# TensorE's matmuls of the head loop in the order of emission, with a head's preparation, maxima and loads moved up

## The chip, the cores and the metric

The kernel runs on one core of a Trainium2 chip. Its engines are TensorE (PE; PEld is its weight load), VectorE (DVE), ScalarE (ACT), GpSimd (POOL) and SyncE (SP), which issues the DMAs here. The metric is the device time of one execution in microseconds (us). Three runs of the kernel before took 1082.86, 1084.32 and 1095.21 us; the median is 1084.32.

## The reference

Three layers follow one another. All inputs are float32; B = 4 batches, H = 8 heads, S = 1152 positions, D = 64.

```
# 1. attention with pooled queries
q_pool = q.reshape(B, H, S // 2, 2, D).mean(axis=3)          # 576 queries a head
attn   = softmax(q_pool @ k^T / 8)                           # sum + 1e-9
x      = (attn @ v), heads side by side                      # (4, 576, 512)
# 2. four attention experts, each token uses two of them
logits = x @ w_gate;  the two largest, softmax over the two
ye     = causal_softmax((x wq[e]) (x wk[e])^T / 8) @ (x wv[e]) @ wo[e]
x      = sum over the two chosen e of weight * ye
# 3. token mix and feed-forward
xk, xr = mu * x + (1 - mu) * x_prev
out    = sigmoid(xr @ w_r) * (relu(xk @ w_k)^2 @ w_v)
```

## The kernel before, in words

**Precision.** Most products are taken in `float32r` with each operand split into a high and a low part (`_h`, `_l`), so one product is three matmuls, or two where high and low parts are stacked along the 128 contraction rows.

**Stage 1, a head.** A head hh (32 of them, eight to a batch) has these pieces.
- `s1_load` (L590 to L598): two DMAs bring q (`qr`, L596) and k (`kr`, L597) into one buffer each.
- `s1_prep` (L610 to L719): POOL adds the query pairs (`qp`, L625); TensorE transposes k (L635, five matmuls) and q (L681, three) into PSUM; ACT or DVE copy the high part out, DVE computes the low part; two steps later eight DMAs lay the parts into KA, KB and QB (L670 to L672, L711). KA, KB, QA and QB have three copies, so head hh + 3 takes over those of head hh.
- `s1_max` (L721 to L742): 15 matmuls of 384 columns (L728), each into a PSUM bank that DVE reduces at once (L730); then `max_finish` (L394 to L405): DVE reduces to `nm` (L397), TensorE transposes it (L402), DVE copies it out (L403) and a DMA on SP (L404) writes it as a row of QB, where the second score matmul subtracts it.
- `s1_job` (L744 to L820): nine steps. The part `qk` of a step is four score matmuls of 288 columns (L758, L759, two pairs) into one of two PSUM tiles `st`; ACT takes the exponential (L766), for two steps of three a copy splits it (L64) and DVE computes the rest (L71). Four steps later the part `pv` multiplies with V (L786, or L793 to L795).
- `s1_vload`, `s1_vsplit`: V is loaded (L602) and split.

**Stage 2, an expert** of the batch before is woven into the heads of the next batch: `s2_vproj`, `s2_qk` (tile `stq`, L348), `s2_max` (L422, L427, five atoms and a `max_finish`), `s2_job` (three steps, scores L467 and L468, products L496) and `s2_out`. They stand as additional steps between those of a head; the positions `p1` to `p6` and `po` in the dictionary G fix where.

**What sets the order.** `drive` (L176 to L206) walks through the 353 steps of the head loop. In step i it emits `qk` of step i, its exponential, the low part of step i - 2, and then, in the gaps before, between and after the `pv` parts of step i - 4, what the tasks have due. A task has a start and an end, both counted in steps, and a list of atoms; `Task.run` emits as many atoms as the elapsed share of the window asks for. Preparation, maxima, loads and the rest are such tasks; their windows come from G (`pr0`, `mx0`, `ld` and others), where x below zero counts from the first step of a head backward. `later(n, f)` emits f at the end of the n-th step from now: `G["nm"]` and `G["nm2"]` are that n for the transposition of the maxima of a head and of an expert.

What is emitted so is a program order only. When the program is compiled, the framework's scheduler simulates the engines and lets an engine take a later instruction where the first in line isn't ready in that simulation. The order in which each engine's queue then stands is fixed; at run time each queue goes through it in that order. PSUM has two tiles `st` of two banks, and four banks (`aux()`) for everything else: transpositions, maxima and the accumulators of the products.

After the head loop a second `drive` (L1274) computes the last batch's experts, and stage 3 follows.

Of the kernel before, what the change touches and what calls it, by code (L numbers as in the profile page):

```python
# [22 lines left out]

P = 128
D = 64
G = {'LAG': 4, 'LO': 2, 'nf1': 2, 'nfx': 1, 'mxA': (0, 5), 'prA': (0.5, 5.0), 'mx0': (-2.0, 7.0), 'mx1': (-2.5, 6.0), 'vl': (0.0, 1.5), 'vs': (5.5, 1.0), 'pr0': (0.5, 5.0), 'pr1': (0.5, 4.0), 'ld': (6.5, 5.5), 'm2': (2.0, 1.5), 'nm': 0, 'nm2': 0, 'dup': 2, 'mid': 1, 'bc': 1, 'end': 9, 'mid2': 2, 'end2': 4, 'spl': 9, 'gate': 8, 'gate2': 2, 'w2': (2, 30), 'w3': (7, 14), 'S0': ('n', 'sv', 'sv', 'n', 'sv', 'sv', 'n', 'sv', 'sv'), 'S1': ('n', 'sv', 'sv', 'n', 'sv', 'sv', 'n', 'sv', 'sv'), 've': 'g', 'kh0': 's', 'kh1': 'v', 'qh0': 's', 'qh1': 's', 'kq': 's', 'kl': 'v', 'rs': 'v', 'rl': 'v', 'ym': 'g', 'yo': 'v', 'LGe': 'v', 'p1': (5, 5, 5, 9), 'p2': (9, 9, 9), 'p3': (2,), 'p4': (9, 9, 9, 9), 'p5': (8, 8, 8, 8), 'p6': (9, 9, 9), 'po': (2, 4, 5, 9), 'add0': 'g', 'add1': 'g', 'xt': 'v', 'u1': 's', 'u2': 's', 'y2': 'v', 'yh': 's', 'yl': 'v', 'xo': 'v', 'v2': 's', 'xh': 's', 'xl': 'v', 'vvh': 's', 'vvl': 'g', 'klo': 'v', 'HB': 3, 'PB': 6, 'blk': 1, 'm2w': 2, 'order': 2, 'kdup': 0, 'L2': 4, 'O2': 1, 'a0': (5.0, 5.0), 'a1': (2.0, 2.5), 'a2': (0.0, 1.0), 'a3': (2.0, 2.0), 'r0': 2, 'NV': 2, 'NF': 2, 'SA': ('n', 'vg', 'sg', 'n', 'sv', 'n', 'sv', 'sv', 'sv'), 'SB': ('n', 'sv', 'sv', 'n', 'vv', 'n', 'sv', 'sv', 'sv'), 'ua': 'v', 'u0': 's', 'xt0': 'v', 'w3d': 8, 'w3q': (3, 27), 'WC': 1, 'kb': 1, 'kst': 1, 'qst': 0, 'CW': 512, 'wt': 'v', 'wl': 'v', 'wa': 'v', 'WB': 1, 'mxg': 2, 'hq': 's', 'hpos': (0, 1, 11, 20)}
NEG = -1.0e30

TINY = 1.17e-9
# [26 lines left out]
def tile_kernel(ctx: ExitStack, tc: tile.TileContext, q, k, v, w_gate, wq, wk, wv, wo,  # L56
                mu_k, mu_r, w_k, w_v, w_r, out):
    nc = tc.nc
    LAG, LO, HB = G["LAG"], G["LO"], G["HB"]
    eng = {"g": nc.gpsimd, "v": nc.vector, "s": nc.scalar}  # L60

    def copy(e, dst, src):
        if e == "s":
            nc.scalar.activation(dst, src, AF.Copy)  # L64
        elif e == "v":
            nc.vector.tensor_copy(dst, src)
        else:
            nc.gpsimd.tensor_scalar(dst, src, 1.0, 0.0, op0=ALU.mult, op1=ALU.add)

    def lo_of(e, dst, src, hi):  # L70
        eng[e].tensor_tensor(dst, src, hi.bitcast(F32), op=ALU.subtract)  # L71
# [82 lines left out]
    def later(n, fn):  # L154
        pending.append((now[0] + n, fn))

    def run_later(everything=False):
        while pending:
            x = min(pending, key=lambda x: x[0])
            if x[0] > now[0]:  # L160
                if not everything:
                    return
                now[0] = x[0]
            pending.remove(x)
            x[1]()
# [3 lines left out]
    def drive(steps, tasks, drain=False):  # L169
        def fill(t):  # L170
            for x in tasks:
                x.run(t)

        for i, st in enumerate(steps):
            now[0] += 1
            if st.qk:  # L176
                st.qk()
            if st.ew:
                st.ew()
            lagged.append(st)  # L180
            if len(lagged) > LO and lagged[-1 - LO].ew2:
                lagged[-1 - LO].ew2()
                lagged[-1 - LO].ew2 = None
            pv = lagged.pop(0).pv if len(lagged) > LAG else ()
            m = len(pv) + 1
            for j in range(m):
                fill(i + (j + 1) / m - 1e-6)
                if j < len(pv):
                    pv[j]()
            run_later()  # L190
        if drain:
            for st in lagged:
                if st.ew2:
                    st.ew2()
                    st.ew2 = None
            while lagged:
                for f in lagged.pop(0).pv:
                    f()
                now[0] += 1
                run_later()  # L200
            run_later(True)
# [36 lines left out]
    def normaliser(U, gate, name):  # L238
# [8 lines left out]
        def mid():  # L247
# [3 lines left out]
            nc.sync.dma_start(scr.rearrange("o (p i) -> (o p) i", p=D), rd)  # L251
            later(G["bc"], bcast)

# [6 lines left out]
    def s2_split(b):  # L260
        def one(p):
            def f():
                copy(G["xh"], XH[:, p], XT[:, p])
                lo_of(G["xl"], XL[:, p], XT[:, p], XH[:, p])
            return f
        return [one(p) for p in range(NP)]

    def s2_vproj(b):
        W = E * D + E

        def make(cs):
# [13 lines left out]
            def ew():  # L285
                for j, c in enumerate(cs):
                    n = TC[c][1]
                    copy(G["v2"], V2[:n, c, :, 0:D], cell["st"][:n, j, : E * D].rearrange("p (e d) -> p e d", e=E))

# [7 lines left out]
    def s2_gate(b):  # L297
# [3 lines left out]
        def f():  # L301
# [22 lines left out]
            def g():  # L324
# [9 lines left out]
                nc.sync.dma_start(GR, gscr.rearrange("e (p i) -> p e i", p=D))  # L334
            later(G["gate2"], g)
        return [f]
# [230 lines left out]
    NK, NV = 3, G["NV"]  # L567

    order = sorted(range(NK), key=lambda i: (i - (B * H)) % NK)
# [6 lines left out]
    NF = G["NF"]  # L576
# [13 lines left out]
    def s1_load(hh):  # L590
        b, h = hh // H, hh % H
        kr = s1a.tile([P, NC * D], F32, tag="kr", name=f"kr{hh}")
        qr = s1a.tile([QW, NQ, 2, D], F32, tag="qr", name=f"qr{hh}")
        raw[hh] = kr, qr
        return [
            lambda: nc.sync.dma_start(qr, q[b, h].rearrange("(c p r) d -> p c r d", p=QW, r=2)),  # L596
            lambda: nc.sync.dma_start(kr, k[b, h].rearrange("(p c) d -> p (c d)", p=P)),  # L597
        ]  # L598

    def s1_vload(hh):  # L600
        b, h = hh // H, hh % H
        return [lambda: nc.sync.dma_start(VF[hh % NF][:, :, 0:D], v[b, h].rearrange("(p c) d -> p c d", p=P))]  # L602
# [116 lines left out]
    def s1_max(hh):  # L719
        i = hh % NK  # L720
        pm = PM[hh % 2]  # L721

        def one(c, g):
            t0, n = TC[c]

            def f():
                ps = aux()
                nc.tensor.matmul(ps[:n, : 3 * P], QA[i][:, t0 : t0 + n], KA[i][:, 3 * g * P : 3 * (g + 1) * P],  # L728
                                 start=True, stop=True)
                nc.vector.tensor_reduce(pm[:n, c, g : g + 1], ps[:n, : 3 * P], axis=AX.X, op=ALU.max)  # L730
            return f

        def some(a, z):
            return [one(c, g) for c in range(a, z) for g in range(3)]

        if hh >= G["nfx"]:
            return some(0, len(TC)) + [lambda: max_finish(pm, QB[i], f"1_{hh}")]

        m = -(-HT // P)
        return some(0, m) + [lambda: first_max(pm, QB[i], 0, m)] + \  # L740
            some(m, len(TC)) + [lambda: first_max(pm, QB[i], m, len(TC))]
# [119 lines left out]
    CW = G["CW"]  # L861
# [68 lines left out]
    steps, tasks = [], []  # L930
# [16 lines left out]
    def at(hh, x):  # L947
        if x < 0:
            return at_[hh][0] + x
        if x >= NC:  # L950
            return at_[hh][NC - 1] + x - NC + 1
        return at_[hh][int(x)] + x - int(x)
# [23 lines left out]
    for hh in range(3):  # L976
        for a in s1_load(hh):
            a()
        if hh < 2:
# [3 lines left out]
            if hh == 0:  # L983
                mx = s1_max(0)
# [7 lines left out]
    for hh in range(NH):  # L992
        z = "0" if hh < H else "1"
        if hh + 1 < NH:
            mx = G["mx" + z] if hh else G["mxA"]
            e = at(hh, mx[1])
            if G["mxg"] and ex_[hh] and hh >= H:
                e = max(e, at_[hh + 1][0] - G["mxg"])
            tasks.append(Task(at(hh, mx[0]), e, s1_max(hh + 1)))
            a = LAG + G["vl"][0]  # L1000
            tasks.append(Task(at(hh, a), at(hh, a + G["vl"][1]), lambda hh=hh: s1_vload(hh + 1)))
            a = LAG + G["vs"][0]
            tasks.append(Task(at(hh, a), at(hh, a + G["vs"][1]), lambda hh=hh: s1_vsplit(hh + 1)))
        if hh + 2 < NH:
            pr = G["pr" + z] if hh else G["prA"]
            tasks.append(Task(at(hh, pr[0]), at(hh, pr[1]), lambda hh=hh: s1_prep(hh + 2)))
        if hh + 3 < NH:
            tasks.append(Task(at(hh, G["ld"][0]), at(hh, G["ld"][1]), lambda hh=hh: s1_load(hh + 3)))
    if G["order"]:
        tasks = tasks[::-1] if G["order"] == 1 else sorted(tasks, key=lambda t: t.start) if G["order"] == 2 else sorted(tasks, key=lambda t: t.end)  # L1010
    n = len(steps)
# [57 lines left out]
    tasks.append(Task(n - 7, n - 6, [wk_open]))  # L1069
    tasks.append(Task(n - 6, n - 5, [lambda: s3_mix(0, "xk")]))  # L1070
    tasks.append(Task(n - 5, n - 1, [wk_part(kt, j) for kt in range(KT) for j in range(2)]))
    drive(steps, tasks, drain=True)
    ph1.close()


# [137 lines left out]
    LAG, LO = G["L2"], G["O2"]  # L1213
    flow, tasks = [], []
# [16 lines left out]
    steps, ix = [], []  # L1231
# [70 lines left out]
```

## Time and profile before

| | |
|---|---|
| median of three runs | 1084.32 us |
| the profiled execution | 1088.18 us |
| its span, from the first to the last instruction | 1086.4 us |
| mean granted TensorE clock | 0.981 |
| TensorE busy | 1024.2 us, 94% |
| DVE busy | 821.5 us, 76% |
| ACT busy | 577.4 us, 53% |
| POOL busy | 192.6 us, 18% |

The profile is of one execution. The time of the execution holds 1.8 us around the span. A busy share says how much of the span an engine had an instruction in work; matmuls overlap, so two of them that start 0.13 us apart can each be shown with 0.3 us. What ended an engine's idle time is inferred from semaphores; where the named instruction was long done, it was another one. The granted clock is a share of 2.4 GHz.

### The profile page before, as it was taken

Reading aid. Unit: us, or ns where it says so; the run is one execution under the profiler, and the core shown is the slowest. Engines: PE = TensorE matmul, PEld = TensorE weight load, DVE = VectorE, ACT = ScalarE, POOL = GpSimd, SP = SyncE. Lnnn points to the kernel's source line nnn. Section 1 sums busy time; section 2 is a strip of 40 time slices with the busy share of each in tenths; the row PEclk is TensorE's granted clock in tenths of the full one; section 3 lists DMA queues with packets and bytes.
Section 4 is the critical chain, followed back from the end, with each engine's and each line's share of the span. In section 5 each row is a group of like instructions: output and inputs, shape, how many; then the busy total and the mean of one; then the engine's idle time right before and its main releaser. Section 6 shows DMA issues by size and latency. Waiting matters only on the chain.

```text
span 1086.4 us, 18206 instructions
## 1 busy us (share of the span) xinstructions
PE 1024.2 (94%) x6480; PEld 891.5 (82%) x6480; DVE 821.5 (76%) x1753; ACT 577.4 (53%) x1011; POOL 192.6 (18%) x277
## 2 busy tenths in 40 slices
PE   5999999999999999999999999998898899999998
PEld 4788988888888888888788888878776688888886
DVE  5898999789899989898898897875876635444442
ACT  4567777457676555766655576663555212222222
POOL 6431121021121112112111111121021001111110
PEclk9899999999999999999999999999898899999999
DMA  4555555455554644644464444157255311111100
GB/s 112 140 138 129 131 133 135 103 120 131 135 126 101 171 117 118 152 124 122 102 164 128 109 120 93 42 171 227 83 181 151 102 42 40 39 40 39 39 21 20
DMA packets 129096, 119.24 MB, mean 110 GB/s; under 512 B 63751, under 2 KB 91358, under 8 KB 129006
## 3 DMA queue, kind: packets, MB, share of 16 engines
q1 hardware_dynamic: 129006, 118.08, 41.7%
q8 instruction: 51, 0.84, 0.3%
q14 instruction: 39, 0.32, 0.1%
HBM read 63.24 MB, written 20.07 MB: 77 GB/s over the span
## 4 chain that ended last, share of the span: by engine, by line
PE 61%; DVE 14%; DMA 13%; ACT 6%; issue 3%; SPq 1%; POOL 0%; DVEq 0%; ACTq 0%; POOLq 0%
PE stw L1135 9%; PE sth L1099 7%; PE bank L728 6%; PE bank L786 5%; PE st L758 5%; PE st L759 5%; PE str L1122 4%; PE stq L348 4%; DMA R<-scr 4%; DVE PM L730 3%; PE bank L795 3%; PE bank L794 3%; PE bank L793 3%; PE bank L496 3%; DMA w3l<-w3st 2%
## 5 line engine op out<-in xcount | busy, mean ns | idle before, releaser
L730 DVE TENSOR_REDUCE PM<-bank 128x1 f32<-128x384 f32 (+1 forms) x480 | 252.5, 544 | 19.5 <-PE bank L728 16.6
L766 ACT ACTIVATE p<-st 128x576 f32<-128x576 f32 x288 | 184.5, 647 | 120.4 <-PE st L759 114.3
L728 PE MATMUL bank<-KA,QA 128*128 128x384 f32 (+1 forms) x480 | 187.6, 403 | 12.0 <-DVE KB L145 4.4
L758 PE MATMUL st<-QA,KA 128*128 128x288 f32 x576 | 177.4, 319 | 3.6 <-ACT p L766 2.7
L759 PE MATMUL st<-QB,KB 65*128 65x288 f32 x576 | 169.0, 309 | 0.1
L71 DVE TENSOR_TENSOR pl<-p,ph 128x576 fp32r<-128x576 f32 x190 | 142.9, 754 | 6.2 <-ACT ph L64 5.3
L64 ACT ACTIVATE ph<-p 128x576 fp32r<-128x576 f32 x190 | 129.6, 684 | 19.9 <-PE bank L794 6.3
L758 PEld LDWEIGHTS st<-QA,KA 128*128 128x128 f32 x576 | 111.9, 195 | 15.5 <-ACT p L766 6.9
L786 PE MATMUL bank<-p,VF 128*65 128x288 f32 x384 | 118.3, 406 | 0.3
L793 PE MATMUL bank<-ph,VV 128*65 128x288 f32 x384 | 116.9, 305 | 0.1
L759 PEld LDWEIGHTS st<-QB,KB 65*128 65x128 f32 x576 | 111.4, 195 | 4.1 <-DMA QB<-mr 0.9
L728 PEld LDWEIGHTS bank<-KA,QA 128*128 128x128 f32 (+1 forms) x480 | 87.3, 185 | 33.2 <-DVE PM L730 8.0
L795 PE MATMUL bank<-pl,VV 128*65 128x288 f32 x384 | 113.8, 296 | 0.0
L794 PE MATMUL bank<-ph,VV 128*64 128x288 f32 x384 | 113.7, 296 | 0.0
L1099 PE MATMUL sth<-xkh,wk 128*128 128x256 f32 x512 | 91.4, 279 | 1.2 <-ACT relu L1106 1.2
L1106 ACT ACTIVATE relu<-sth 128x512 f32<-128x512 f32 x32 | 17.5, 596 | 123.2 <-PE sth L1099 122.5
L1099 PEld LDWEIGHTS sth<-xkh,wk 128*128 128x128 f32 x512 | 78.8, 188 | 1.8 <-ACT relu L1106 1.4
L625 POOL TENSOR_TENSOR qp<-qr 96x384 f32<-96x384 f32 x31 | 37.7, 1217 | 239.7 <-PE bank L681 160.4
L482 POOL TENSOR_SCALAR_AFFINE_SELECT p<-p 128x128 f32<-128x128 f32 (+1 forms) x96 | 36.4, 411 | 204.6 <-ACT p L474 192.9
L1099 PE MATMUL sth<-xkl,wk 128*128 128x256 f32 x256 | 71.5, 279 | 0.0
L71 POOL TENSOR_TENSOR VV<-VF,VV 128x576 fp32r<-128x576 f32 x32 | 44.5, 1390 | 146.2 <-ACT VV L64 92.8
L1107 DVE TENSOR_TENSOR relu<-relu 128x512 f32<-128x512 f32 x32 | 20.9, 688 | 57.9 <-ACT relu L1106 57.9
(205 smaller groups left out, 2275.8 us busy)
## 6 DMA issues: line engine op xcount, KB each, us to landing
KA<-sk SPq DMA_DIRECT2D x60, 160.0 KB
qr<-in_q_dram SPq DMA_DIRECT2D x32, 288.0 KB
kr<-in_k_dram SPq DMA_DIRECT2D x32, 288.0 KB
VF<-in_v_dram SPq DMA_DIRECT2D x32, 288.0 KB
KA<-sk SPq DMA_DIRECT2D x60, 128.0 KB
R<-scr SPq DMA_DIRECT2D x48, 144.0 KB
w3h<-w3st SPq DMA_DIRECT2D x20, 256.0 KB
w3l<-w3st SPq DMA_DIRECT2D x20, 256.0 KB
```

The costliest lines, as they stand in the source:

```text
L64: nc.scalar.activation(dst, src, AF.Copy)
L71: eng[e].tensor_tensor(dst, src, hi.bitcast(F32), op=ALU.subtract)
L728: nc.tensor.matmul(ps[:n, : 3 * P], QA[i][:, t0 : t0 + n], KA[i][:, 3 * g * P : 3 * (g + 1) * P], start=True, stop=True)
L730: nc.vector.tensor_reduce(pm[:n, c, g : g + 1], ps[:n, : 3 * P], axis=AX.X, op=ALU.max)
L758: nc.tensor.matmul(st[:, n, :HT], KA[i][:, ks], QA[i][:, cs], start=True, stop=False)
L759: nc.tensor.matmul(st[:, n, :HT], KB[i][0 : D + 1, ks], QB[i][0 : D + 1, cs], start=False, stop=True)
L766: nc.scalar.activation(pt, st[:, :, :HT], AF.Exp, scale=1.0 / 16.0)
L786: nc.tensor.matmul(a[: D + 1, :HT], VF[hh % NF][:, c], cell["p"][:, n], start=c == 0, stop=c == NC - 1)
L793: nc.tensor.matmul(a[: D + 1, :HT], vh, ph[:, n], start=c == 0, stop=False)
L794: nc.tensor.matmul(a[:D, :HT], vl, ph[:, n], start=False, stop=False)
L795: nc.tensor.matmul(a[: D + 1, :HT], vh, pl[:, n], start=False, stop=c == NC - 1)
L1099: nc.tensor.matmul(st[:, f // 2, f % 2 * GT : (f % 2 + 1) * GT], w[kt][:, fs], x[:, kt], start=i == 0, stop=i == 3 * KT - 1)
```

## The change

Two things change. First, the head loop's `drive` stands inside `tc.manual_schedule(engines={PE})`: the scheduler keeps TensorE's instructions of that loop in the order of emission. The other engines are scheduled as before, and so is all that comes before and after the loop. Second, windows in G move, and the first three heads get windows of their own.

```diff
-    'mx0': (-2.0, 7.0), 'mx1': (-2.5, 6.0),
+    'mx0': (-4.5, 4.5), 'mx1': (-4.5, 4.5), 'mxB': (-1.0, 5.5), 'mxC': (-3.5, 5.0),
-    'pr0': (0.5, 5.0), 'pr1': (0.5, 4.0),
+    'pr0': (-3.0, 1.0), 'pr1': (-3.0, 1.0), 'prB': (-1.5, 2.0),
-    'ld': (6.5, 5.5),
+    'ld': (1.5, 1.0), 'ldA': (5.5, 5.0), 'ldB': (2.5, 2.0),
-    'm2': (2.0, 1.5), 'nm': 0, 'nm2': 0,  'mxg': 2,
+    'm2': (2.0, 3.0), 'nm': 1, 'nm2': 1,  'mxg': 4,
...
-            mx = G["mx" + z] if hh else G["mxA"]
+            mx = G["mx" + z] if hh > 2 else G["mx" + "ABC"[hh]]
...
-            pr = G["pr" + z] if hh else G["prA"]
+            pr = G["pr" + z] if hh > 1 else G["prB"] if hh else G["prA"]
...
-            tasks.append(Task(at(hh, G["ld"][0]), at(hh, G["ld"][1]), lambda hh=hh: s1_load(hh + 3)))
+            ld = G["ld"] if hh > 1 else G["ldB"] if hh else G["ldA"]
+            tasks.append(Task(at(hh, ld[0]), at(hh, ld[1]), lambda hh=hh: s1_load(hh + 3)))
...
-    drive(steps, tasks, drain=True)
+    with tc.manual_schedule(engines={mybir.EngineType.PE}):
+        drive(steps, tasks, drain=True)
```

Worked out from the windows and `drive`, the pieces of a head are emitted so many steps ahead of its own first score step (a head of batch 0, heads 5 to 8; and, for later batches, where additional steps stand between, the range):

| piece | before, batch 0 | after, batch 0 | before, later | after, later |
|---|---|---|---|---|
| loads | 21 | 26 | 25 to 32 | 30 to 37 |
| preparation, first to last | 18 to 15 | 21 to 18 | 21 to 26, 18 to 23 | 24 to 29, 21 to 26 |
| its DMAs | 14, 13 | 17, 16 | 17 to 22 | 20 to 25 |
| first maximum | 11 | 14 | 12 to 16 | 14 to 18 |
| last maximum | 4 | 6 | 4 or 5 | 6 |
| transposition of the maxima | 3 | 5 | 3 or 4 | 4 or 5 |

For an expert the maxima end a step earlier, and their transposition stays at the same step, three before the expert's first scores.

## Rows read from the trace of the kernel before

**Rows 1.** The page, part 1: busy time and share of the span by engine.
```profile
PE 1024.2 (94%) x6480; PEld 891.5 (82%) x6480; DVE 821.5 (76%) x1753; ACT 577.4 (53%) x1011; POOL 192.6 (18%) x277
```

**Rows 2.** Windows: length; busy (count) of PE, PEld, DVE, ACT, POOL; clock, DMA.
```profile
0.00:34.90 34.90, 22.04 (x84) 17.75 (x85) 19.63 (x49) 18.84 (x41) 22.67 (x36) 0.91 0.47 110
34.90:98.30 63.40, 58.90 (x368) 50.32 (x367) 56.54 (x114) 38.87 (x70) 18.88 (x20) 0.97 0.60 144
98.30:180.40 82.10, 81.23 (x541) 72.27 (x540) 78.16 (x158) 60.93 (x108) 14.04 (x10) 1.00 0.51 125
180.40:715.50 535.10, 518.67 (x3436) 451.89 (x3435) 472.80 (x1073) 336.00 (x596) 83.05 (x112) 0.99 0.49 121
```

**Rows 3.** Groups by line; after the bar busy us, mean ns, idle before.
```profile
L758 PE MATMUL st<-QA,KA 128*128 128x288 f32 x576 | 177.4, 319 | 3.6 <-ACT p L766 2.7 <-DVE QA L145 0.5
```

**Rows 4.** Windows of the half clock in the loop; columns as in rows 2.
```profile
28.12:34.93 6.81, 6.28 (x23) 5.91 (x24) 4.30 (x9) 4.49 (x9) 3.42 (x5) 0.52 0.43 107
86.17:89.57 3.40, 3.38 (x15) 3.12 (x16) 2.92 (x7) 1.53 (x4) 0.00 (x0) 0.53 0.32 72
...
721.06:724.45 3.39, 3.39 (x11) 2.50 (x12) 2.78 (x6) 2.54 (x5) 2.16 (x4) 0.53 0.65 203
```

**Rows 5.** Timeline of TensorE at the start: start, duration, instruction, [idle before <-releaser].
```profile
17.86 0.44 PE L759 MATMUL st<-QB,KB 65*128 65x288 f32 x1
...
24.25 0.29 PE L759 MATMUL st<-QB,KB 65*128 65x288 f32 x1
27.07 0.41 PE L728 MATMUL bank<-KA,QA 128*128 128x384 f32 x1 [2.52 <-DVE KB L145]
28.65 1.45 PE L728 MATMUL bank<-KA,QA 128*128 128x384 f32 x3 [1.17 <-DVE KB L145]
```

**Rows 6.** Timeline of TensorE at 86 us.
```profile
86.19 0.30 PE L635 MATMUL bank<-ident,kr 128*64 128x128 f32 x1 [1.88 <-DVE sk L145]
```

**Rows 7.** Timeline of TensorE at 492 us.
```profile
492.12 0.51 PE L793 MATMUL bank<-ph,VV 128*65 128x288 f32 x1
493.49 0.37 PE L468 MATMUL st<-QB,KB 65*128 65x288 f32 x1 [0.86 <-DMA QB<-mr]
```

**Rows 8.** Timeline of TensorE at 594 and 721 us.
```profile
594.14 0.40 PE L348 MATMUL stq<-XH,wqk_h 128*128 128x288 f32 x1 [2.10 <-ACT p L766]
...
594.54 0.42 PE L728 MATMUL bank<-KA,QA 128*128 128x384 f32 x1
...
720.94 0.40 PE L758 MATMUL st<-QA,KA 128*128 128x288 f32 x1 [2.18 <-ACT p L766]
```

**Rows 9.** Tile nm: TensorE's idle time before its users, us in total, times.
```profile
  DVE nm L397: 6.1, 13
```

**Rows 10.** Waits of TensorE from 34.9 to 735 us: total, times, longest.
```profile
PE bank L728 <- DVE PM L730: 3.9, 7, 1.1
PE bank L402 <- DVE nm L397: 1.9, 4, 1.0
PE bank L635 <- DMA kr<-in_k_dram: 1.0, 1, 1.0
PE st L468 <- DMA QB<-mr: 0.9, 1, 0.9
```

**Rows 11.** Windows of the heads 4 and 16; columns as in rows 2.
```profile
98.30:114.40 16.10, 16.10 (x111) 14.62 (x109) 15.76 (x33) 12.59 (x25) 2.98 (x2) 1.00 0.53 127
350.40:374.90 24.50, 24.00 (x164) 21.55 (x163) 24.04 (x44) 14.30 (x25) 2.90 (x2) 1.00 0.60 162
```

**Rows 12.** Waits of SP's queue: total, times, longest.
```profile
SPq L404 <- DVE PM L730: 51.1, 24, 7.2
```

**Rows 13.** Timeline of TensorE: two product matmuls in a row.
```profile
214.92 0.29 PE L794 MATMUL bank<-ph,VV 128*64 128x288 f32 x1
215.05 0.30 PE L795 MATMUL bank<-pl,VV 128*65 128x288 f32 x1
```

**Rows 14.** Timeline of TensorE: an expert's maximum inside a product group.
```profile
216.81 0.33 PE L422 MATMUL bank<-KA,QA 128*128 128x128 f32 x1
```

More of the change, by code (lines that the diff above doesn't have):

```diff
@@ L25 @@
 D = 64
-G = {'LAG': 4, 'LO': 2, 'nf1': 2, 'nfx': 1, 'mxA': (0, 5), 'prA': (0.5, 5.0), 'mx0': (-2.0, 7.0), 'mx1': (-2.5, 6.0), 'vl': (0.0, 1.5), 'vs': (5.5, 1.0), 'pr0': (0.5, 5.0), 'pr1': (0.5, 4.0), 'ld': (6.5, 5.5), 'm2': (2.0, 1.5), 'nm': 0, 'nm2': 0, 'dup': 2, 'mid': 1, 'bc': 1, 'end': 9, 'mid2': 2, 'end2': 4, 'spl': 9, 'gate': 8, 'gate2': 2, 'w2': (2, 30), 'w3': (7, 14), 'S0': ('n', 'sv', 'sv', 'n', 'sv', 'sv', 'n', 'sv', 'sv'), 'S1': ('n', 'sv', 'sv', 'n', 'sv', 'sv', 'n', 'sv', 'sv'), 've': 'g', 'kh0': 's', 'kh1': 'v', 'qh0': 's', 'qh1': 's', 'kq': 's', 'kl': 'v', 'rs': 'v', 'rl': 'v', 'ym': 'g', 'yo': 'v', 'LGe': 'v', 'p1': (5, 5, 5, 9), 'p2': (9, 9, 9), 'p3': (2,), 'p4': (9, 9, 9, 9), 'p5': (8, 8, 8, 8), 'p6': (9, 9, 9), 'po': (2, 4, 5, 9), 'add0': 'g', 'add1': 'g', 'xt': 'v', 'u1': 's', 'u2': 's', 'y2': 'v', 'yh': 's', 'yl': 'v', 'xo': 'v', 'v2': 's', 'xh': 's', 'xl': 'v', 'vvh': 's', 'vvl': 'g', 'klo': 'v', 'HB': 3, 'PB': 6, 'blk': 1, 'm2w': 2, 'order': 2, 'kdup': 0, 'L2': 4, 'O2': 1, 'a0': (5.0, 5.0), 'a1': (2.0, 2.5), 'a2': (0.0, 1.0), 'a3': (2.0, 2.0), 'r0': 2, 'NV': 2, 'NF': 2, 'SA': ('n', 'vg', 'sg', 'n', 'sv', 'n', 'sv', 'sv', 'sv'), 'SB': ('n', 'sv', 'sv', 'n', 'vv', 'n', 'sv', 'sv', 'sv'), 'ua': 'v', 'u0': 's', 'xt0': 'v', 'w3d': 8, 'w3q': (3, 27), 'WC': 1, 'kb': 1, 'kst': 1, 'qst': 0, 'CW': 512, 'wt': 'v', 'wl': 'v', 'wa': 'v', 'WB': 1, 'mxg': 2, 'hq': 's', 'hpos': (0, 1, 11, 20)}
@@ new lines @@
+G = {'LAG': 4, 'LO': 2, 'nf1': 2, 'nfx': 1, 'mxA': (0, 5), 'mxB': (-1.0, 5.5), 'mxC': (-3.5, 5.0), 'prA': (0.5, 5.0), 'prB': (-1.5, 2.0), 'mx0': (-4.5, 4.5), 'mx1': (-4.5, 4.5), 'vl': (0.0, 1.5), 'vs': (5.5, 1.0), 'pr0': (-3.0, 1.0), 'pr1': (-3.0, 1.0), 'ldA': (5.5, 5.0), 'ldB': (2.5, 2.0), 'ld': (1.5, 1.0), 'm2': (2.0, 3.0), 'nm': 1, 'nm2': 1, 'dup': 2, 'mid': 1, 'bc': 1, 'end': 9, 'mid2': 2, 'end2': 4, 'spl': 9, 'gate': 8, 'gate2': 2, 'w2': (2, 30), 'w3': (7, 14), 'S0': ('n', 'sv', 'sv', 'n', 'sv', 'sv', 'n', 'sv', 'sv'), 'S1': ('n', 'sv', 'sv', 'n', 'sv', 'sv', 'n', 'sv', 'sv'), 've': 'g', 'kh0': 's', 'kh1': 'v', 'qh0': 's', 'qh1': 's', 'kq': 's', 'kl': 'v', 'rs': 'v', 'rl': 'v', 'ym': 'g', 'yo': 'v', 'LGe': 'v', 'p1': (5, 5, 5, 9), 'p2': (9, 9, 9), 'p3': (2,), 'p4': (9, 9, 9, 9), 'p5': (8, 8, 8, 8), 'p6': (9, 9, 9), 'po': (2, 4, 5, 9), 'add0': 'g', 'add1': 'g', 'xt': 'v', 'u1': 's', 'u2': 's', 'y2': 'v', 'yh': 's', 'yl': 'v', 'xo': 'v', 'v2': 's', 'xh': 's', 'xl': 'v', 'vvh': 's', 'vvl': 'g', 'klo': 'v', 'HB': 3, 'PB': 6, 'blk': 1, 'm2w': 2, 'order': 2, 'kdup': 0, 'L2': 4, 'O2': 1, 'a0': (5.0, 5.0), 'a1': (2.0, 2.5), 'a2': (0.0, 1.0), 'a3': (2.0, 2.0), 'r0': 2, 'NV': 2, 'NF': 2, 'SA': ('n', 'vg', 'sg', 'n', 'sv', 'n', 'sv', 'sv', 'sv'), 'SB': ('n', 'sv', 'sv', 'n', 'vv', 'n', 'sv', 'sv', 'sv'), 'ua': 'v', 'u0': 's', 'xt0': 'v', 'w3d': 8, 'w3q': (3, 27), 'WC': 1, 'kb': 1, 'kst': 1, 'qst': 0, 'CW': 512, 'wt': 'v', 'wl': 'v', 'wa': 'v', 'WB': 1, 'mxg': 4, 'hq': 's', 'hpos': (0, 1, 11, 20)}
```

## The prediction

> **What bounds the kernel now.** I read the page's busy shares first [rows 1]: TensorE (PE) is busy 1024.2 of 1086.4 us, the vector engine (DVE) 821.5, the scalar engine (ACT) 577.4. TensorE carries the time, and little idle time is left to be won. Then the windows by stage [rows 2], since the change touches one stage only, the loop over the 32 heads. Where a head starts is counted off in the score matmuls L758, 18 to a head, 576 in all [rows 3]. The reader is to see four numbers there. In the start (0 to 34.9 us) TensorE does 22.0 us of work. In the heads 1 to 3 (34.9 to 98.3) it is idle 63.4 - 58.9 = 4.5 us, in the heads 4 to 8 (98.3 to 180.4) 82.1 - 81.2 = 0.9 us, in the heads 9 to 30 (180.4 to 715.5) 535.1 - 518.7 = 16.4 us: 21.8 us in all. And in that last stretch DVE is busy 472.8 of 535.1 us, 88%, so a second engine stands close behind. The heads 4 to 8 are the measure of what the loop can do: 99% busy.
>
> The third view is the granted clock. Five stretches of the loop have it at half, 1.2 GHz in place of 2.4 [rows 4]: one of 6.8 us at 28.1 and four of 3.4 us, of which the first at 86.2 and the last at 721.1 are shown; the two between begin at 495.8 and 594.8, within 2.3 us after the waits of [rows 7] and the first of [rows 8]. A half-clock stretch of 3.4 us does 1.7 us less of matmul work. What came before each is read from the timeline: TensorE stood still between 24.25 and 27.07 with one matmul and a second wait of 1.17 us after it [rows 5]; at 86.19 it had waited 1.88 us for DVE [rows 6]; at 493.49 it had waited, 0.86 us of that put down to the DMA of the row of maxima [rows 7]; at 594.14 it had waited 2.10 us and at 720.94 2.18 us for ACT's exponential [rows 8]. So a long wait is paid twice here, as idle time and as slow matmuls.
>
> **The change, part by part.** All prices are against the profiled execution, 1088.18 us (span 1086.4 and 1.8 around it); the median of the three runs shown, 1084.32, lies 3.9 lower, and I give my number on the median.
>
> *The order itself* removes no instruction and adds none: the same matmuls are issued in another order. In the trace the present order shows itself where a maximum's matmul (L728) stands inside a group that the program emits in one piece: in [rows 8] it follows a `stq` whose group (L348, 24 matmuls) goes on behind it. By itself that costs nothing; what it may cost is that an unready matmul now holds everything behind it. I bound that part by part.
>
> *Transposition of the maxima a step later* (nm, nm2 from 0 to 1). L402 now makes TensorE idle 6.1 us in 13 waits for DVE's reduction `nm` [rows 9]; the longest on TensorE's own list is 1.0 us [rows 10]. A step takes about 1.8 us (16.1 us for a plain head of nine steps, [rows 11]), so the later slot covers them. Bounds 0 and -6.1; I take **-4**, because some of these waits lie under a matmul still running. What is late next is the row of maxima in QB, whose SP queue entry (L404) already waits 51.1 us in 24 times for DVE [rows 12]. For the head stage nothing is lost there, since all 15 maxima move up by two or three steps and the transposition by one or two; for the expert stage the slot of the transposition stays where it was.
>
> *Maxima earlier.* The waits of a score matmul for that row (0.9 us in [rows 10]) go: **-0.9**. The waits of L728 for a bank that DVE still reads, 3.9 us in 7 times on TensorE's list [rows 10], depend on DVE's pace and not on the slot: 0, with bounds of 3.9 either way.
>
> *Preparation and loads earlier.* POOL's sum `qp`, the eight transpositions, the copies of ACT and DVE and eight DMAs a head move up three or four steps; the two loads move up about five, so that load to sum grows from three steps to five or more (from head 5 on). TensorE waited 1.0 us for kr once [rows 10]: **-1**. These DMAs pass other heads' entries on SP's queue, and the sum passes the splits of V on POOL's; a load that moves up and must wait for its buffer holds what stands behind it, the rows of maxima among them, and these in turn the scores. The cover is the three steps, some 5 us, between a head's maxima and its scores; if it goes, the price is a wait of the size of [rows 6].
>
> *Isolated waits.* The wait at 86.19 is for a bank in the preparation, at 493.49 for the row of maxima, at 594.14 for ACT. With 1.7 us of half clock each they cost 3.7, 2.9 (a start-to-start of 1.37 us where 0.13 is normal, so 1.2 lost [rows 7, 13]) and 4.0 us, 10.6 together. The change can remove all or none. At 86 the transposition comes three steps earlier, at 493 the reduction one step; at 594 TensorE only has that one maximum more to do before the wait, 0.2 us. I take the first two, **-6.6**. The one at 720.94 has no maxima near it: 0.
>
> *The first heads.* Now the score matmuls of head 0 run ahead of the maxima of head 1: from 17.86 to 24.25 TensorE works through some twenty of them, and the first L728 of head 1 comes at 27.07 [rows 5]. In emission order only the first step's four may go before it. About 20 matmuls of 0.13 us (132 ns from start to start, [rows 13]) or 0.24 at half clock are put off: +2.6 to +4.8, less what they fill of the waits behind (1.17 and 2.52 us there): 0 at best if the maxima start no earlier, -2 if ACT and DVE, freed of that head's exponentials, finish head 1 sooner. I take **+1**.
>
> *New waits.* Twelve times the expert stage begins with its own maxima (L422) and scores (L467). At 216.81 such a maximum stands inside a product group, behind five product matmuls that the program emits after it, 5 x 0.13 = 0.7 us [rows 13, 14]. If its data were not ready before, TensorE now waits up to 0.7 us each time: bounds 0 and 12 x 0.7 = +8.4; TensorE's list has no wait of L422 now and only 0.9 us of L468 [rows 10], so I take a sixth of a microsecond each, **+2**.
>
> Sum: -4 - 0.9 - 1 - 6.6 + 1 + 2 = -9.5, so 1074.8 on the median; I say **1075**. Small gaps that no list names add nothing: a matmul takes 151 ns of busy time in the heads 9 to 30 (518.67 us by 3436) and 150 in the heads 4 to 8 (81.23 by 541) [rows 2].
>
> **A rule against the change.** The rows show TensorE waiting with work behind it. The Trainium skill, PSUM — Partial Sum Buffer, section Engine vs sequencer instructions, says that matmuls start and complete in program order and only a weight load overlaps a running matmul. By that, whatever is emitted first and is not ready stops the engine, and a scheduler that sets it back is worth keeping; the trace agrees: nothing passed the transposition that waited until 86.19. What it would cost here is the third rival.
>
> **The rivals.** *All waits go.* The idle time of the heads 1 to 30, 21.8 us, and 1.7 us in each of three half-clock stretches, 5.1, are all there is on the list: 1084.3 - 26.9 = **1057**. For it speak the heads 4 to 8, which run at 99%; against it DVE, which in 350.4 to 374.9 is busy 24.0 of 24.5 us [rows 11], so that part of the loop cannot shrink whatever TensorE does.
> *Nothing changes.* The heads 4 to 8 run at 99% in the order as it is, and in the others DVE sets the pace; waits only change their names: **1083 to 1087**.
> *Slower: an unready matmul of the expert stage holds the queue.* Its place is L422 and L467, twelve times. If each wait reaches 2 us, the clock falls behind it as it did at 86, 594 and 721, and each costs 2 + 1.7 = 3.7 us: +44, less the 12.5 of the terms with a minus: **1116**. It decides from about 1 us a wait on, where twelve of them eat the gain; with six in twelve it is 1094. Beside this stands the Trainium skill, TensorE: Matmul & The Clock Gate, section HAM oscillation — how this bites in real kernels, by which waits for data bring the clock down so that the next matmuls start slow; the trace agrees in the four places named.
>
> **How the numbers follow.** The forecast (1064 to 1082) has 0.42, all waits gone 0.20, nothing changed 0.20, slower 0.18. Two per cent, about what a measurement of this kernel can tell from no change, is 21.7 us: 1062.6 and 1106. Faster takes the first rival and a little of the forecast, 0.23; slower takes the upper half of the third, 0.12; the rest 0.65. The range reaches from under the first rival to the middle of the third: 1054 to 1097.
>
> **What would show it.** Right: L402 no longer in the list of waits, TensorE idle under 17 us between the starts of head 1 and head 31, two of the stretches at 86, 496 and 595 back at full clock. Wrong: L422, L467 or L728 with more idle time than now, a half-clock stretch behind an expert's scores, DVE over 90% with no gain, or the first maximum of head 1 later than 27 us.

## The result, and the profile after

The changed kernel took 1094.68 us (median of 20 runs), the kernel before 1083.93 us on the same chip: the ratio is 1.0092, 95% interval 1.0073 to 1.0112. It is slower by 0.9%; I had predicted 0.9% faster. Run again later on another chip it gave 1.0120 (1.0086 to 1.0154). One kernel further below, the emission order with short reductions and the later output, was profiled at a granted clock of 0.56, and no view of it is used.

The profiled execution has a span of 1092.3 us, 5.9 more than before. (The kernel before was profiled in an execution of 1088.18 us, 4.3 above its median of 1083.93, the changed one at its median; so the two profiles show about 6 of the 10.7 us between the medians.) First the page's busy time by engine.

```profile
PE 1024.0 (94%) x6480; PEld 884.7 (81%) x6480; DVE 826.6 (76%) x1753; ACT 583.8 (53%) x1011; POOL 187.8 (17%) x277
```

TensorE does the same work in the same busy time [rows 1], so the 5.9 us between the profiles are idle time. Where they lie, the windows by stage show, cut at the starts of the heads 1, 4, 9 and 31 as in [rows 2] (length; busy time and count of PE, PEld, DVE, ACT, POOL; clock, DMA).

```profile
0.00:43.50 43.50, 29.33 (x130) 22.45 (x131) 27.95 (x69) 22.94 (x49) 23.80 (x37) 1.00 0.54 129
43.50:97.50 54.00, 51.85 (x331) 43.85 (x330) 50.35 (x102) 36.76 (x64) 17.65 (x18) 1.00 0.62 143
97.50:181.30 83.80, 82.14 (x540) 71.34 (x539) 80.04 (x158) 61.93 (x106) 11.96 (x10) 1.00 0.53 131
181.30:723.60 542.30, 518.85 (x3428) 449.59 (x3428) 473.52 (x1066) 339.15 (x596) 79.47 (x112) 0.99 0.45 117
```

Head 4 starts 0.8 us earlier than before. The heads 4 to 8 take 1.7 us longer, the heads 9 to 30 7.2 us: there TensorE is idle 542.3 - 518.9 = 23.4 us where it was 16.4, with equal busy time. Over the heads 1 to 30 it is idle 27.3 us (before 21.8).

The waits of TensorE (total, times, longest) from 34.9 to 735 us, the stretch of [rows 10]:

```profile
PE bank L728 <- DVE sk L145: 3.2, 4, 1.7
PE bank L728 <- DVE PM L730: 3.2, 7, 1.2
PE st L758 <- ACT p L766: 2.9, 1, 2.9
PE bank L402 <- DVE nm L397: 2.4, 4, 0.8
PE bank L681 <- ACT U L134: 2.2, 1, 2.2
PE bank L728 <- ACT U L134: 1.9, 2, 1.0
PE bank L402 <- DVE PM L730: 1.5, 2, 0.8
PE bank L422 <- DVE PM L730: 1.3, 5, 0.3
PE bank L422 <- DMA KA<-KA: 1.2, 2, 1.0
PE bank L635 <- DVE PM L730: 1.2, 5, 0.5
...
PE bank L793 <- DVE sk L145: 0.9, 3, 0.5
```

The reader is to look at the first name. The waits of matmuls that write one of the four single banks (`bank`) add up to 24.6 us in 52 times over the whole list, where before they were 11.6 in 17; those on all other tiles fall from 10.7 to 4.5. The releaser is often not the producer of the matmul's operands: `sk` and U are copies that empty a bank, and so mostly is L730. By these names TensorE mostly waits for banks that VectorE and ScalarE have still to empty.

How one such wait looks, in the timeline (start, duration, instruction, [idle before <-releaser]):

```profile
454.48 0.29 PE L759 MATMUL st<-QB,KB 65*128 65x288 f32 x1
455.22 0.67 ACT L885 ACTIVATE w3st<-w3st 128x512 f32<-128x512 f32 x1 [3.33 <-DMA w3st<-in_moe_w_k_dram]
...
455.79 0.64 ACT L766 ACTIVATE p<-st 128x576 f32<-128x576 f32 x1
...
456.32 0.49 ACT L134 ACTIVATE U<-bank,epsc 65x288 f32<-65x288 f32 x1
...
456.95 0.44 PE L681 MATMUL bank<-ident,qp 96*128 96x96 f32 x3 [2.18 <-ACT U L134]
457.18 0.35 PE L793 MATMUL bank<-ph,VV 128*65 128x288 f32 x1
```

ScalarE's queue stood behind a weight of stage 3 that was still arriving; so the exponential and then the copy out of a product bank came late, and the transposition L681 of a head much further on had no bank. The product L793 behind it starts 0.23 us after L681 with no wait listed of its own. Then come 3.4 us at half clock, as after the wait at 330.95 (0.96 us) and the one at 402.14 (1.22):

```profile
331.80:335.20 3.40, 3.40 (x15) 3.05 (x14) 2.53 (x5) 1.23 (x2) 0.46 (x3) 0.50 0.02 6
403.50:406.90 3.40, 3.40 (x15) 3.40 (x16) 3.12 (x6) 0.99 (x2) 0.00 (x0) 0.50 0.13 27
458.10:461.50 3.40, 3.40 (x12) 2.50 (x11) 3.06 (x6) 2.42 (x5) 0.44 (x1) 0.50 0.39 94
```

The stretches at 86, 496, 595 and 721 [rows 4] are gone; three others stand elsewhere.

A long wait is not always followed by such a stretch. At 729.41 TensorE had waited 2.9 us for ScalarE (the third line of the list above), and the clock stayed at full speed. In the second run of the same kernel the wait of L681 is 2.2 us again, and the heads 1 to 30 have no half-clock stretch at all:

```profile
727.00:735.00 8.00, 5.59 (x32) 4.35 (x33) 5.81 (x11) 7.01 (x12) 3.23 (x8) 1.00 0.68 248
```
```profile
PE bank L681 <- ACT U L134: 2.2, 1, 2.2
43.40:717.30 673.90, 647.99 (x4295) 560.81 (x4295) 604.71 (x1324) 437.44 (x765) 109.49 (x139) 1.00 0.47 122
```

### The profile page after: what moved, and what is told of

The parts are those of the page before. It is cut to its first block, busy times and chain, and to the rows that moved or that the text cites. A ratio compares the mean times of both kernels' runs of the same rounds, so it can differ in the third digit from the quotient of the medians.

```text
span 1092.3 us, 18217 instructions
## 1 busy us (share of the span) xinstructions
PE 1024.0 (94%) x6480; PEld 884.7 (81%) x6480; DVE 826.6 (76%) x1753; ACT 583.8 (53%) x1011; POOL 187.8 (17%) x277
## 5 line engine op out<-in xcount | busy, mean ns | idle before, releaser
L730 DVE TENSOR_REDUCE PM<-bank 128x1 f32<-128x384 f32 (+1 forms) x480 | 254.3, 546 | 27.3 <-PE bank L728 23.6
L728 PE MATMUL bank<-KA,QA 128*128 128x384 f32 (+1 forms) x480 | 187.0, 398 | 15.6 <-DVE KB L145 4.3
L759 PE MATMUL st<-QB,KB 65*128 65x288 f32 x576 | 163.9, 299 | 0.0
L71 DVE TENSOR_TENSOR pl<-p,ph 128x576 fp32r<-128x576 f32 x190 | 148.3, 781 | 13.1 <-ACT ph L64 11.1
L793 PE MATMUL bank<-ph,VV 128*65 128x288 f32 x384 | 117.5, 306 | 1.9 <-DVE sk L145 0.9
L728 PEld LDWEIGHTS bank<-KA,QA 128*128 128x128 f32 (+1 forms) x480 | 87.9, 185 | 36.4 <-DVE PM L730 8.1
L786 PE MATMUL bank<-p,VF 128*65 128x288 f32 x384 | 114.6, 409 | 0.7 <-DVE PM L409 0.6
L71 POOL TENSOR_TENSOR VV<-VF,VV 128x576 fp32r<-128x576 f32 x32 | 44.7, 1396 | 200.2 <-ACT VV L64 175.0
L625 POOL TENSOR_TENSOR qp<-qr 96x384 f32<-96x384 f32 x31 | 34.5, 1113 | 217.1 <-PE bank L681 162.7
L786 PEld LDWEIGHTS bank<-p,VF 128*65 128x65 f32 x384 | 51.9, 139 | 20.4 <-DVE PM L409 1.2
```

The costliest lines, as they stand in the source:

```text
L759: nc.tensor.matmul(st[:, n, :HT], KB[i][0 : D + 1, ks], QB[i][0 : D + 1, cs], start=False, stop=True)
L786: nc.tensor.matmul(a[: D + 1, :HT], VF[hh % NF][:, c], cell["p"][:, n], start=c == 0, stop=c == NC - 1)
L793: nc.tensor.matmul(a[: D + 1, :HT], vh, ph[:, n], start=c == 0, stop=False)
```

## The experiments

Two theories first. **O:** the order itself costs, since an unready matmul now holds ready ones, and the moved windows win a part back. **W:** the moved windows cost, and the order is harmless. Ratios are to the kernel before on the same chip, with 95% intervals.

**The order alone.**
```
 G as before
+    with tc.manual_schedule(engines={mybir.EngineType.PE}):
         drive(steps, tasks, drain=True)
```


> The kernel before with TensorE's matmuls of the head loop in the order of emission, and the old windows. Theory O (the order costs: an unready matmul holds the queue, and the earlier windows only make up for a part of it): clearly slower than the changed kernel, over 1105 us, since the 41 or so transpositions of the maxima that now are set back by 1 to 5 us in the queue each hold TensorE. Theory W (the earlier windows cost: they lay DVE's work and the PSUM banks badly over the steps, and the order is harmless): 1084 to 1090 us, close to the kernel before.


Measured: 1123.59 us, 1.0421 (1.0390 to 1.0451). In its list of waits one line stands out:

```profile
PE bank L402 <- DVE nm L397: 27.4, 30, 2.8
```

The transposition of the maxima is emitted right behind the last maximum, and in emission order TensorE waits there in 30 of 43 cases. Before, it was 1.9 us in 4 [rows 10]: the scheduler had set 41 of the 43 back behind later matmuls (by the order in the two traces).

**The windows alone.**
```
 G as after
-    with tc.manual_schedule(engines={mybir.EngineType.PE}):
-        drive(steps, tasks, drain=True)
+    drive(steps, tasks, drain=True)
```


> The changed kernel with the scheduler free again to reorder TensorE: only the windows of preparation, maxima and loads differ from the kernel before. Theory O: 1080 to 1087 us, no slower than the kernel before. Theory W: 1090 to 1097 us, as slow as the changed kernel.


Measured: 1071.04 us, 0.9934 (0.9908 to 0.9960), faster than both kernels and below the range of either theory. The same heads 9 to 30 as a window:

```profile
177.30:706.10 528.80, 513.97 (x3433) 451.08 (x3432) 482.35 (x1071) 336.26 (x598) 81.10 (x112) 0.99 0.47 120
```

14.8 us idle here, and 13.6 us in 21 waits on the single banks in its list of waits. With the same windows the emission order has 24.6 us in 52. O holds and W falls: the order costs 4.2% with the old windows and 1.0092 - 0.9934 = 1.6% with the new ones.

One thing more differs between such twins. The scheduler arranges the other engines' queues anew too: by the order in the two traces with the new windows, some 320 of VectorE's instructions and 110 of ScalarE's stand behind one that they precede in the other. The wait at 456.95 is a case: in the free order the same copy of the weight stands two exponentials later in ScalarE's queue and waits for nothing.

```profile
445.10 0.68 ACT L885 ACTIVATE w3st<-w3st 128x512 f32<-128x512 f32 x1
```

No run holds these other orders fixed, so what is called the price of the order holds their share too.

**The later transposition alone, free order.**
```
-'nm': 0, 'nm2': 0
+'nm': 1, 'nm2': 1     (kernel before otherwise)
```


> The kernel before with the transposition of the maxima emitted one step later (nm and nm2 from 0 to 1) and nothing else. My prediction priced this at -4 us, so 1080. Theory O: 1080 to 1084, since the scheduler sets the transposition back by 2 to 3 us anyway. Theory W: the same; if it is slower than 1088, the later row of maxima is what costs, under either order.


Measured: 1074.66 us, 0.9961 (0.9941 to 0.9981); by this ratio 4.2 us less.

**Maxima back in their old windows**, with the emission order, and below with the free order.
```
 kernel after, but
+'mx0': (-2.0, 7.0), 'mx1': (-2.5, 6.0), 'mxB': (-2.0, 7.0), 'mxC': (-2.0, 7.0), 'mxg': 2
```


> The changed kernel (order of emission, preparation and loads early, transposition a step later) with the windows of the maxima as before. Theory O: slower than the changed kernel, 1097 to 1110 us, as the row of maxima comes two steps later and holds the scores. Theory W with the maxima as the cause: 1083 to 1089 us. If it stays at 1093 to 1096, the maxima's place is not the cause.


Measured: 1129.75 us, 1.0477 (1.0446 to 1.0507), slower than either theory had it. Its longest line of waits:

```profile
PE st L759 <- DMA QB<-mr: 28.5, 23, 3.1
```

The row of maxima comes late and the second score matmul waits for it with all else behind.

> The free twin of the strict kernel with the old windows of the maxima (preparation and loads early, transposition a step later, scheduler free). O2: the scheduler hides the late row of maxima behind other matmuls, 1069 to 1078, some 53 us under its strict twin (1130). If the late row itself were what costs there: over 1100. It also shows whether the early maxima are worth anything to a free order: if this one is at 1071, they are not.


Measured: 1077.92 us, 1.0002 (0.9983 to 1.0020). The free order hides the same late row: 4.7% lie between the twins. The early maxima are worth 1.0002 - 0.9934 = 0.7% to the free order and 1.0477 - 1.0092 = 3.9% to the emission order. And against the later transposition alone (0.9961) the early preparation and loads, with the old maxima, cost the free order 0.4%: the intervals 0.9941 to 0.9981 and 0.9983 to 1.0020 lie just apart, on two chips.

**Which heads pay?** The head loop's `drive` cut at head 9, one part with the emission order.
```
+    cut = at_[9][0]
     with tc.manual_schedule(engines={mybir.EngineType.PE}):
-        drive(steps, tasks, drain=True)
+        drive(steps, tasks, hi=cut)
+    drive(steps, tasks, drain=True, lo=cut)
```


> The new windows; order of emission for the steps of the heads 0 to 8 only, the rest free. Theory O2 (the order costs some tenths of a microsecond in nearly every head, wherever a matmul has to wait for a PSUM bank or for DVE and others stand ready behind it): between the free and the strict form of the new windows (1071 and 1095), by the starts of head 9 in their profiles (181.3 against 177.3) 4 us over the free one, 1073 to 1077. Rival S (only the expert stage's matmuls, L422 and L467, hold the queue): 1070 to 1072, as the free one. Rival H (it is head 0, whose scores no longer run ahead): 1085 or more.


Measured: 1078.06 us, 1.0000 (0.9984 to 1.0017).

> The new windows; order of emission from the first step of head 9 on, the heads 0 to 8 free. O2: the rest of the cost, 1087 to 1092. S: all of it, 1093 to 1096. H: 1070 to 1076.


Measured: 1084.83 us, 1.0064 (1.0039 to 1.0089). Against the free order's 0.9934 the nine heads without experts cost 0.7%, the other 23 1.3%. Both lie outside what I had expected of O2 (1073 to 1077 and 1087 to 1092 us), and together they give 2.0%, more than the 1.6% of the whole. But neither the first heads alone nor the experts alone pay: the price is spread.

**The transposition yet a step later** (`'nm': 2`).


> The changed kernel with the transposition of a head's maxima two steps behind their last one in place of one. O2 with the transposition still the largest single wait (L402 makes TensorE idle some 4 us in all and its weight load more): 1089 to 1092. If the row of maxima then comes too late for the scores: over 1097. If these waits only move to the next matmul that lacks a bank: 1093 to 1096.


Measured: 1093.28 us, 1.0141 (1.0116 to 1.0165): no gain. Against the first run of the changed kernel (1.0073 to 1.0112) it is slower, against the second (1.0086 to 1.0154) no difference can be told.

**Is it VectorE's pace?** O2, the spread form of O, says that the banks come free too late because VectorE is behind. So each maximum's reduction reads a third of what TensorE writes, with TensorE's work left as it is.
```
-nc.vector.tensor_reduce(pm[:n, c, g : g + 1], ps[:n, : 3 * P], ...)
+nc.vector.tensor_reduce(pm[:n, c, g : g + 1], ps[:n, : P], ...)
```


> The changed kernel (emission order, new windows), but each maximum's reduction L730 reads 128 of the 384 columns that TensorE has written, so the maxima leave two thirds of the scores out; TensorE's matmuls are the same. L730 takes 546 ns now, 480 times; I estimate 0.28 us for the short one (the copy L403 of 128 columns takes 271 ns), so a bank of PSUM comes free 0.27 us earlier and VectorE does some 128 us less. Theory O2 (the order costs because a matmul whose PSUM bank VectorE has not yet emptied holds those behind it): TensorE idle over heads 1 to 30 falls from 27.3 to under 15 us, and the gap to the free twin falls from 1.6% of the time to under 0.8%: 1055 to 1068. Rival F (the order costs at fixed latencies between engines, whatever VectorE's load): the gap to the twin stays at 15 to 20 us, idle time over 20.


Measured: 1073.59 us, 0.9958 (0.9936 to 0.9980). The reduction's own row (duration min/median/max, before it was 547 in the median):

```profile
L730 DVE TENSOR_REDUCE PM<-bank x480: 218/284/293, 9.7 to 697.7; 128x1 f32<-128x128 f32 x128, 64x1 f32<-64x128 f32 x32
```

> The free twin: the new windows, the short reductions (two thirds of the scores left out of the maxima), TensorE's order chosen by the scheduler. Its own twin with whole reductions gave 0.9934 of the kernel before, with TensorE idle 17.3 us in heads 1 to 30. Theory O2: the scheduler had already filled most of the waits for banks, so it gains less than the kernel in emission order does: 1055 to 1065. Rival F: it gains as much as that one, and stays 15 to 20 us below it: 1040 to 1052.


Measured: 1064.38 us, 0.9878 (0.9855 to 0.9900). Relieved of 126 us of VectorE's work (480 times 547 - 284 ns), the emission order gains 1.3 to 1.6% and the free order 0.6%; the gap halves, from 1.6 to 0.8%. Two expectations were missed: the emission order's time lies above 1055 to 1068 us, and TensorE is idle 21.1 us in the heads 1 to 30 (27.3 before the relief) where I had under 15. But the free twin is idle 16.5 us there (17.3 before), so the difference between the twins falls from 10.0 to 4.6 us. So about half of the price is VectorE's, and half was still open. The short reduction frees a bank sooner and takes work off VectorE at once; which of the two it is, no run separates.

**The other half.** In the emission order's profile of that pair, head 16 is 30.8 us long, in the free twin 25.9. Waits in it, its window and the half-clock stretch:

```profile
PE sto L548 <- ACT YH L64: 1.9, 1, 1.9
PE sto L548 <- DVE YL L71: 1.6, 1, 1.6
```
```profile
346.80:377.60 30.80, 26.51 (x164) 24.10 (x163) 21.27 (x45) 15.63 (x26) 2.55 (x2) 0.89 0.52 152
353.70:360.50 6.80, 5.82 (x23) 5.54 (x24) 4.71 (x10) 1.38 (x3) 0.00 (x0) 0.50 0.40 110
```

An expert's output waits for its operands. Its first steps were put one or two steps later in both twins.
```
-'po': (2, 4, 5, 9)
+'po': (4, 5, 7, 9)
```


> Emission order, new windows, short reductions (two thirds of the scores left out of the maxima), and the expert's output steps (L548) at positions (4, 5, 7, 9) of their head in place of (2, 4, 5, 9). There the matmuls waited 1.9 and 1.6 us for YH and YL in head 16, and 6.8 us at half clock followed. If that place holds the rest of the order's price: head 16 falls from 30.8 to about 26 us, the ratio to the kernel before from 0.9958 to about 0.991 to 0.993. If the rest is spread over many places: 0.995 to 0.997.


Measured: 1070.13 us, 0.9899 (0.9878 to 0.9920), a larger gain than either reading had; head 16 was not measured.

> The free twin of the same. There L548 waited 1.6 us in that head and the clock stayed up, so there is little to win: 0.986 to 0.988 of the kernel before. The gap between the twins is 0.4% by the one reading (one place), 0.8% by the other (spread).


Measured: 1064.44 us, 0.9850 (0.9826 to 0.9873). The emission order gains 0.6% by the move, and its intervals before and after lie apart; the free order gains 0.3%, within its intervals. The gap is now 0.5%, with an interval of 0.2 to 0.8: that this one place held 0.3% of the 0.8 is likely and not shown.

The same move with whole reductions:

> Whole reductions, nothing left out: the new windows, TensorE's order chosen by the scheduler, the expert's output steps at (4, 5, 7, 9). With the output at (2, 4, 5, 9) it gave 0.9934, TensorE waiting 1.9 us for L548. If the output's place is worth as much as with short reductions (0.9878 to 0.985), 0.990 to 0.992; if VectorE's pace covers it, 0.993 to 0.995.


Measured: 1071.28 us, 0.9932 (0.9906 to 0.9957).

> The changed kernel, whole reductions, with the expert's output steps at (4, 5, 7, 9). It gave 1.0092 and 1.012 with them at (2, 4, 5, 9), with only 1.4 us of waits for L548. If the output holds half of the order's price here too: 1.001 to 1.005. If VectorE's pace covers it: 1.008 to 1.012.


Measured: 1089.24 us, 1.0096 (1.0064 to 1.0127). Nothing is won in either. In the changed kernel L548 waits only 1.4 us in all, so that place is late only once VectorE is relieved; what a kernel waits for depends on what it waited for before. The gap is 1.6% again, with both twins on one chip.

**A middle course, and the changed kernel again.**
```
 free order, G as after, but
+'mx0': (-3.5, 5.5), 'mx1': (-3.5, 5.0), 'pr0': (-1.0, 2.5), 'pr1': (-1.0, 2.5), 'ld': (4.0, 3.0)
```


> An attempt at a version that beats both: TensorE's order chosen by the scheduler, the windows of later heads half-way between the old and the new ones (preparation (-1, 2.5), maxima (-3.5, 5.5 and 5.0), loads (4, 3)). The new windows gave 0.9934 under the free order, the old maxima with new preparation 1.0002. If the gain is all in the row of maxima's lead, which here shrinks from two steps more than before to one, it gives 0.993 to 0.998; if the early preparation and loads cost something (they have more copies to wait for), 0.988 to 0.993.


Measured: 1073.54 us, 0.9962 (0.9946 to 0.9978): between, as the first reading had it. It moves preparation, maxima and loads together, so it does not tell what the preparation costs alone.

> The changed kernel once more, unaltered, on the same chip as these: 1.007 to 1.012 of the kernel before, as the first time. If it gives 1.013 or more, the 1.0141 of the kernel with the transposition yet a step later was the chip's and not the step's.


Measured: 1089.78 us, 1.0120 (1.0086 to 1.0154).

## Why the prediction was wrong

**The step that failed** is the first of the part by part: of the order itself I wrote that "by itself that costs nothing", and bounded the rest by two places, +1 for the first heads and +2 for the experts' maxima and scores. Measured, the order costs 4.2% alone and 1.6% with the new windows, 17 us where I had 3. With the moves' -7 this makes the +10 us that were measured. The two places are not where the 17 us lie. In the free order with the same windows head 4 starts at 95.1 us, so the order costs 2.4 us up to there, where I had +1 (it starts 0.8 us earlier than before all the same, with the wait at 86 gone). L422 now waits 2.5 us where it had no line before, but it waits 2.0 us in the free order with the same windows too:

```profile
PE bank L422 <- DVE PM L730: 2.0, 5, 0.5
```

What I missed is all other places. By the order in the traces of the kernel before and of the order alone, the scheduler had set back some 920 matmuls behind later ones; with the new windows it is some 580, with the short reductions some 180, and the price of the order falls with it, 4.2, 1.6, 0.8%. I saw three such places ([rows 5], the maximum inside the `stq` group in [rows 8], the one in [rows 14]) and asked what they cost, not what they save: 99% busy in the heads 4 to 8 was read as the measure of the loop, but it was in part the scheduler's work. With the emission order these heads are idle 1.7 us in place of 0.9, and the heads 9 to 30 23.4 in place of 16.4. Against the free order with the same windows, 11 of the 17 us show as small waits for one of four banks (24.6 us in 52 against 13.6 in 21), and 4.9 as a longer busy time in the heads 9 to 30 (518.85 against 513.97).

**The moves** were predicted at -4 - 0.9 - 1 - 6.6 = -12.5 and gave -7.1 us under the free order (0.66% of 1079.42; interval -9.9 to -4.3), so the sign was right and the size too large. The parts, again under the free order: the later transposition alone gave -4.2 where I had -4; the early preparation and loads +4.4 (0.9961 to 1.0002) where I had -1; the early maxima -7.3 (1.0002 to 0.9934) where I had -0.9 and a share of the isolated waits (the last two from runs on two chips, each to some 3 us). That the first agrees is partly luck, because [rows 9] adds two queues, and in that run L402 still waits 0.9 us, so only 1.0 of the 4.2 us is there. This is who waited for `nm` in the kernel before:

```profile
  PEld bank L402: 4.3, 9
  PE bank L402: 1.9, 4
```

6.1 is the weight load's waits and the matmul's together. Of the matmul's own idle time only 1.9 us was there. In the changed kernel the two are

```profile
  PEld bank L402: 3.4, 5
  PE bank L402: 2.4, 4
```

so in emission order the later slot only held the line, against 27.4 us without it.

**Isolated waits, -6.6:** the waits at 86 and 493 did go with their half-clock stretches, and so did those at 594 and 721, where I had 0. But others came (456.95, 402.14, 330.95), and a wait of 2.9 us stands at 729. In these traces such waits are not removed one at a time: they come up again where a late copy meets the matmul that needs its bank. Nor is a long wait always paid twice, as I had it: behind the 2.9 us at 729 and, in the second run, behind the 2.2 us of L681 the clock stayed at full speed.

**The rival that was to be slower** had the right mechanism, an unready matmul that holds the queue, and the wrong place. I gave it L422 and L467 only, twelve times; the waits of the score matmuls L467 and L468 fell from 3.5 us, of which I had read only the 0.9 of L468, to 0.2. That its middle value, 1094, is the measured time is a coincidence. The rule weighed against the change was the better guide (the Trainium skill, PSUM — Partial Sum Buffer, section Engine vs sequencer instructions: matmuls start in program order). The trace agrees: behind the transposition L681, which waited until 456.95, the product L793 starts 0.23 us later without a wait of its own. I should have applied it to each operation that the scheduler had moved, not to two.

**DVE as the bound** I had used against the best case alone. It is about half of what makes the order expensive: relieved of 126 us, half of the gap is gone. The other half stays open: with short reductions and the later output 0.5% remain, 5 us, whose places were not tried. In the profiles of the short pair 2.2 us of the gap arise before head 1 starts (at 40.3 against 38.1 us), which I only read and didn't test.

**The signs I had named** spoke clearly. TensorE idle under 17 us between the heads 1 and 31: it was 27.3. L402 out of the list: it is in it. L728 and L422 with more idle time than now: both. One sign of being right did come, the stretches at 86, 496 and 595 back at full clock; and two of being wrong did not, DVE over 90% (it is at 87% in the heads 9 to 30) and a later first maximum of head 1 (24.43 us).

## What to carry to other kernels

Before an engine is held to the order of emission, count how many of its instructions the scheduler has moved and ask of each group what wait it covers; waits that a profile does not list may be hidden, not absent. An emission order is only as good as the slack that every operand and every PSUM bank has at its slot, so give that slack (here the early maxima and the later transposition), measure it under the free order, and keep it there: the windows alone gave 0.9934. And when a row gives the idle time for a tile, see which queue waited: a weight load's wait is not the matmul's.

## What the hardware showed that I had not expected

A VectorE operation can take over twice as long beside one of GpSimd. The same subtraction `pl` of 128x576 takes 0.74 us at 423.60 and 1.83 at 421.31, started while GpSimd's L71 was running:

```profile
420.88 1.65 POOL L71 TENSOR_TENSOR VV<-VF,VV 128x576 fp32r<-128x576 f32 x1 [8.88 <-ACT VV L64]
...
421.31 1.83 DVE L71 TENSOR_TENSOR pl<-p,ph 128x576 fp32r<-128x576 f32 x1
...
423.60 0.74 DVE L71 TENSOR_TENSOR pl<-p,ph 128x576 fp32r<-128x576 f32 x1
```
```profile
75.02 1.28 POOL L148 TENSOR_TENSOR wo_l<-wst,wo_h 128x512 fp32r<-128x512 f32 x1
75.31 1.60 DVE L71 TENSOR_TENSOR pl<-p,ph 128x576 fp32r<-128x576 f32 x1
```

In both cases the subtraction ends 0.61 us after GpSimd's operation does (423.14 against 422.53, 76.91 against 76.30), as if it stood until the other was done. Not every meeting does this, but the 152 of the 190 that lie beside no operation of GpSimd all take 0.68 to 0.76 us.

Over the kernel the mean of that group rose, before and after (after the bar busy us, mean ns):

```profile
L71 DVE TENSOR_TENSOR pl<-p,ph 128x576 fp32r<-128x576 f32 x190 | 142.9, 754 | 6.2 <-ACT ph L64 5.3
```
```profile
L71 DVE TENSOR_TENSOR pl<-p,ph 128x576 fp32r<-128x576 f32 x190 | 148.3, 781 | 13.1 <-ACT ph L64 11.1 <-PE st L759 0.6
```

That is 5.4 us more, about the 5.1 us by which VectorE's busy time rose; which operations meet depends on when GpSimd's come, and no run here took the meeting away. And a reduction from PSUM of a third of the columns takes 284 ns in place of 547: by these two points 1.03 ns a column over some 150 ns that do not depend on them.
